# Batch 1's q and k loads, cut by runs into two or three transfers each

## The chip, the cores and the metric

The kernel runs on one core of one Trainium2 chip. The number that is compared is device time in microseconds for one execution; smaller is better. The core has a matrix engine (TensorE, PE in the profile; its weight loads are listed apart as PEld), a vector engine (VectorE, DVE), a scalar engine (ScalarE, ACT), GpSimd (POOL) and a sync engine (SyncE, SP). SP does no arithmetic here: it issues DMA transfers, one after the other, in the order of the program. Sixteen DMA engines move the data; every transfer in this trace reports its landing with sixteen signals on one semaphore, one from each DMA engine.

## What is computed

Inputs are q, k and v (8 batches, 8 heads, 576 positions, 64 wide, float32) and two weight matrices, `w_in` (512 x 2048) and `w_out` (2048 x 512).

```
scores = (q @ k.T) / 8 - slope[head] * |i - j|      for 0 <= i - j < 128, else masked
attn   = softmax(scores) @ v                         per batch and head
x      = attn, heads side by side                    4608 tokens x 512
h      = x @ w_in
out    = (h * clip(h + 3, 0, 6) / 6) @ w_out         4608 x 512, float32
```

## The kernel before

The heads of a batch are taken in pairs, so a batch has four groups g (batch 0 is g 0 to 3, batch 1 is g 4 to 7). For each group the kernel needs q and k transposed (64 x 576 per head) in bf16, computes scores for blocks of 128 by 128 on and beside the diagonal, exponentiates them on ACT, multiplies by v, normalises on DVE and transposes the result into `xT`. A block of 512 tokens of `xT` then goes through `moe_up` (640 matmuls in all at line 451, ACT at 470, DVE at 471) and `moe_down` (560 matmuls at line 501). The whole program is written out by hand: every engine's instructions stand in the order of the calls in `first_batch`, `second_batch` and `segment`, and pieces of the MoE work are put between the attention steps by `fill`.

The loads of q and k come in several forms. Batch 0 uses `load_run` (line 92): one transfer of 128 rows per group and tensor. Batches 1 and 2, and k of batch 3, use `load_double` (line 98). One call covers four heads of one tensor (half a batch, `dp` 0 or 1) with two transfers, e = 0 and e = 1. Each transfer has 64 runs of nine neighbouring positions for two heads; a run of one head is 9 x 64 float32 = 2304 bytes, contiguous in memory, and goes to one partition: partition 2a + i holds run a of the i-th of the two heads. So one transfer is 128 rows of 2304 bytes, 288 KB. Later batches and all of v use `load_tokens` (line 112), whose rows are 256 bytes.

What stands around batch 1's loads, all in `first_batch`:

- SP's queue is: q of batch 0 (k of batch 0 goes through ACT's queue), the five v transfers of batch 0, then batch 1's eight q and k transfers in the order k and q of dp 0, k and q of dp 1 (line 594), then the five v transfers of batch 1 (`load_tokens(1, "v")`), then batch 2's q and k (line 611).
- The transfers of SP and ACT share eight landing semaphores in rotation. In the trace a transfer that reuses a semaphore is issued only after the transfer that had it eight places earlier has landed: the first v transfer of batch 1 has the semaphore of the first k transfer, which landed at 18.76 us, and it is issued at 18.77 us; the second is issued at 21.27 us, after the landing of the second k transfer at 21.26 us.
- POOL casts batch 1's q and k to bf16 (`prepare_double`, line 227), eight casts in the order of the loads, each when its transfer has landed. Between the first and the second stands the load of the second quarter of `w_in` (`second_w_in`), which goes through POOL's own DMA queue. After the eighth cast POOL issues the third and fourth quarter (`load_w_in(2)`, `load_w_in(3)`).
- PE transposes the cast tiles in `wide_double` (line 254): q of dp 0 before the first full MoE block starts, k of dp 0 within it, k and q of dp 1 at the beginning of groups 4 and 5. The up projection of the first block (`fill`, line 451) goes through the quarters of `w_in` in order.
- Batch 1's v is cast on POOL by `cast_tokens(1, "v")` (lines 187 and 190) after group 5. Behind it on POOL stand the masks of groups 6 and 7 (line 354), the four loads of `w_out` (line 171) and batch 2's casts (`prepare_double(2, ...)`), whose first tiles PE transposes at line 242.

Of the kernel before, what the change touches and what calls it, by code (L numbers as in the profile page):

```python
# [18 lines left out]
def kernel(  # L19
# [10 lines left out]
    B, H, S, D = q.shape  # L30
# [10 lines left out]
    RP, RT = 64, 9  # L41
# [35 lines left out]
    ldbuf = [held.tile([128, NQ * H * D], FP32, name=f"ldbuf{i}") for i in range(4)]  # L77
# [7 lines left out]
    src_of = {"q": q, "k": k, "v": v}  # L85
# [4 lines left out]
    def load_run(g, nm, eng):  # L90
# [2 lines left out]
                      in_=src_of[nm][b, 2 * hp:2 * hp + 2, :, :].rearrange(  # L93
                          "e (p t) d -> (e p) (t d)", t=RT))

    def load_double(b, dp, nm, eng):
        for e in range(2):
            eng.dma_start(out=ldbuf["qk".index(nm)][:, ds((2 * dp + e) * RT * D, RT * D)],  # L98
                          in_=src_of[nm][b, ds(4 * dp, 4), :, :].rearrange(
                              "(i e) (a t) d -> e a i (t d)", e=2, t=RT)[e])  # L100
# [457 lines left out]
    def first_batch():  # L558
# [32 lines left out]
        for dp in range(2):  # L591
            for nm in "kq":
                load_double(1, dp, nm, nc.sync)
# [15 lines left out]
        for dp in range(2):  # L609
            for nm in "kq":  # L610
                load_double(2, dp, nm, nc.sync)
# [6 lines left out]
    def second_batch():  # L618
# [22 lines left out]
        for dp in range(2):  # L641
            load_double(3, dp, "k", nc.sync)
# [121 lines left out]
```

## Time and profile before

| | |
|---|---|
| device time, median of 2 runs | 325.73 us (325.59 to 325.86) |
| span of the profiled execution, first to last instruction | 325.3 us |
| TensorE clock granted | 1.000 |
| PE busy | 314.0 us (97%) |
| ACT / DVE / POOL busy | 198.4 / 173.7 / 141.4 us |
| batch 1's q and k: first issue, last landing | 12.52 us, 28.30 us |
| one such issue on SP: min / median | 0.54 / 0.6 us |

The runs are 0.3 to 0.6 us above the span: that is what lies around the first and the last instruction. Times within the kernel are counted from the start of the span. In lists of instructions an entry gives start and length, engine, line, operation and tiles; the bracket at the end is the time for which the engine stood idle before it and what ended that wait. In lists of waits the numbers are the total, how often, and the longest.

### The profile page before, as it was taken

How to read it: one execution, taken by the hardware profiler on the slowest of the kernel's cores; microseconds unless marked ns; L12 is line 12 of the kernel's file. 1: busy time of each engine (PE TensorE's matmuls, PEld its weight loads, DVE VectorE, ACT ScalarE, POOL GpSimd, SP SyncE). 2: the span in 40 equal slices, each digit the busy share in tenths (PEclk: the TensorE clock that was granted, in tenths of full speed). 3: DMA queues.
4: the chain of work that ended last, by engine and by line, in shares of the span. 5: the costliest groups of instructions: out<-in, count | busy, mean ns of one | idle time of the engine just before them, and what ended most of it. 6: DMA issues, size and time to landing. Idle time of an engine off the chain costs nothing.

```text
span 325.3 us, 7087 instructions
## 1 busy us (share of the span) xinstructions
PE 314.0 (97%) x2763; PEld 168.4 (52%) x2763; DVE 173.7 (53%) x338; ACT 198.4 (61%) x339; POOL 141.4 (43%) x249
## 2 busy tenths in 40 slices
PE   7869999999999999999999999999999999999996
PEld 6555465455555555555667655554554444444443
DVE  7657565554445655565555555554565544445510
ACT  4748877877766666666666666666666344244411
POOL 7446393495395566636663666462342000000000
PEclk9999999999999999999999999999999999999999
DMA  7999999799999999799989986931114100000112
GB/s 274 197 328 180 224 298 191 167 257 218 202 254 176 238 212 208 178 222 217 194 146 229 198 207 138 202 107 64 40 36 55 64 33 34 32 32 34 61 41 91
DMA packets 128065, 51.08 MB, mean 157 GB/s; under 512 B 115616, under 2 KB 119968, under 8 KB 128032
## 3 DMA queue, kind: packets, MB, share of 16 engines
q1 hardware_dynamic: 122800, 44.54, 63.4%
q0 software_dynamic: 4224, 4.19, 8.2%
q10 hardware_dynamic: 1008, 1.90, 1.6%
q8 instruction: 21, 0.34, 0.5%
q14 instruction: 12, 0.10, 0.1%
HBM read 36.70 MB, written 9.44 MB: 142 GB/s over the span
## 4 chain that ended last, share of the span: by engine, by line
PE 82%; DMA 7%; ACT 4%; SPq 3%; DVE 1%; issue 1%; POOL 0%; ACTq 0%
PE ops L501 37%; PE hps L451 34%; DMA ldbuf<-in_q_dram 3%; PE scd L296 2%; PE av L391 2%; DMA w_in_sb<-in_moe_w_in_dram 2%; SPq L112 2%; PE av L383 2%; DMA ldbuf<-in_k_dram 2%; ACT r L470 2%; SPq L98 1%; PE sco L328 1%; ACT xT L438 1%; PE ops L482 1%; PE tb L432 1%
## 5 line engine op out<-in xcount | busy, mean ns | idle before, releaser
L471 DVE SCALAR_TENSOR_TENSOR gbuf<-r,hps 128x512 bf16<-128x512 f32 x144 | 98.5, 686 | 104.8 <-ACT r L470 104.8
L470 ACT ACTIVATE r<-hps,bias 128x512 f32<-128x512 f32 x144 | 99.0, 689 | 82.1 <-PE hps L451 81.8
L451 PE MATMUL hps<-xT,w_in_sb 128*128 128x512 bf16 (+1 forms) x640 | 146.2, 358 | 2.7 <-DMA w_in_sb<-in_moe_w_in_dram 1.9
L501 PE MATMUL ops<-w_out_sb,gbuf 128*128 128x512 bf16 x560 | 138.6, 379 | 0.0
L451 PEld LDWEIGHTS <-w_in_sb 128*128 128x128 bf16 x640 | 58.8, 98 | 56.4 <-DMA w_in_sb<-in_moe_w_in_dram 3.0
L501 PEld LDWEIGHTS <-gbuf 128*128 128x128 bf16 x560 | 52.0, 98 | 56.0
L354 POOL TENSOR_SCALAR_AFFINE_SELECT pd<-pd 128x512 bf16<-128x512 bf16 x48 | 30.0, 633 | 58.4 <-ACT pd L351 58.4
L364 POOL TENSOR_SCALAR_AFFINE_SELECT po<-po 128x512 bf16<-128x512 bf16 x48 | 30.3, 634 | 25.5 <-ACT po L361 24.7
L351 ACT ACTIVATE pd<-scd,bias_d 128x512 bf16<-128x512 f32 x48 | 32.1, 685 | 2.6 <-POOL vbuf L187 2.6
L361 ACT ACTIVATE po<-sco,bias_o 128x512 bf16<-128x512 f32 x48 | 33.2, 692 | 0.0
L510 DVE COPY osb<-ops 128x512 f32<-128x512 f32 x33 | 22.7, 688 | 18.7 <-PE ops L501 18.1
L194 POOL CAST tbuf<-ldbuf 128x512 bf16<-128x512 f32 (+1 forms) x45 | 25.6, 611 | 3.9 <-DMA qTb<-tbuf 3.1
L402 DVE TENSOR_TENSOR avs<-av,rc 128x384 bf16<-128x384 f32 (+1 forms) x48 | 23.6, 491 | 1.6
L391 PEld LDWEIGHTS <-pd 128*128 128x128 bf16 x192 | 14.3, 97 | 8.2 <-issue 0.9
L438 ACT COPY xT<-tb 128x576 bf16<-128x576 bf16 x13 | 8.3, 638 | 16.7 <-PE tb L432 16.7
L383 PE MATMUL av<-vbuf,po 128*128 128x65 bf16 x192 | 18.0, 193 | 0.0
L391 PE MATMUL av<-vbuf,pd 128*128 128x65 bf16 x192 | 17.3, 194 | 0.3 <-ACT kTb L244 0.3
L187 POOL CAST vbuf<-ldbuf 128x1024 bf16<-128x1024 f32 x14 | 14.3, 1040 | 5.2 <-DMA ldbuf<-in_v_dram 5.2
L383 PEld LDWEIGHTS <-po 128*128 128x128 bf16 x192 | 14.3, 98 | 3.0 <-DVE avs L402 0.5
L227 POOL CAST pr<-ldbuf 128x576 bf16<-128x576 f32 x20 | 12.8, 668 | 6.6 <-PE tb L432 2.5
L367 ACT ACTIVATE p4buf<-sco,bias_d 128x64 bf16<-128x64 f32 x48 | 15.7, 327 | 0.0
L296 PEld LDWEIGHTS <-kTb 64*128 64x128 bf16 x256 | 7.2, 94 | 14.1 <-issue 10.6
(96 smaller groups left out, 227.3 us busy)
## 6 DMA issues: line engine op xcount, KB each, us to landing
out_dram<-osb SPq DMA_DIRECT2D x33, 256.0 KB, 2.4
ldbuf<-in_v_dram SPq DMA_DIRECT2D x32, 256.0 KB, 5.6
ldbuf<-in_q_dram SPq DMA_DIRECT2D x20, 256.0 KB, 4.7
ldbuf<-in_k_dram SPq DMA_DIRECT2D x16, 256.0 KB, 4.8
ldbuf<-in_q_dram SPq DMA_DIRECT2D x12, 288.0 KB, 7.8
ldbuf<-in_k_dram SPq DMA_DIRECT2D x12, 288.0 KB, 8.1
w_in_sb<-in_moe_w_in_dram POOLq DMA_DIRECT2D x4, 512.0 KB, 9.8
w_out_sb<-in_moe_w_out_dram POOLq DMA_DIRECT2D x4, 512.0 KB, 11.3
```

The lines of the kernel that those rows point to most:

```text
L194: nc.gpsimd.tensor_copy(out=tbuf[:m, :, j, :], in_=s[:m, j, :, :].rearrange("p (i e) d -> p i (e d)", e=2))
L351: nc.scalar.activation(out=pd[:, e, :, :].rearrange("p j c -> p (j c)"), in_=sc[:, e, :], func=ACT.Exp, bias=bias_d[:, h:h + 1], scale=scale)
L354: nc.gpsimd.affine_select(out=pd[:, e, :, :], in_=pd[:, e, :, :], pattern=[[0, 4], [1, 128]], channel_multiplier=-1, base=0, compare_op=AL ...
L361: nc.scalar.activation(out=po[:, e, :, :].rearrange("p j c -> p (j c)"), in_=sc[:, e, :], func=ACT.Exp, bias=bias_o[:, h:h + 1], scale=scale)
L364: nc.gpsimd.affine_select(out=po[:, e, :, :], in_=po[:, e, :, :], pattern=[[0, 4], [-1, 128]], channel_multiplier=1, base=-1, compare_op=A ...
L383: nc.tensor.matmul(out_av, lhsT=po[:, e, qt % 4, :], rhs=vb[:, qt - 1, h, :], start=True, stop=False)
L391: nc.tensor.matmul(out_av, lhsT=d, rhs=vb[:, qt, h, :], start=(qt == 0), stop=True)
L402: nc.vector.tensor_tensor(out=st[g, "avs"][:, qts[0]:qts[0] + nq, :, :], in0=av[:, 0:nq, :, 0:D], in1=rc[:, 0:nq, :, :].to_broadcast([128, ...
L451: nc.tensor.matmul(hps[:, lo:hi], lhsT=w_in_sb[:, ks, ts(ms, 128)], rhs=xT[:, ks, ds(src, hi - lo)], start=(ks == 0), stop=(ks == n_ks - 1))
L470: nc.scalar.activation(out=r6, in_=hps, func=ACT.Relu, bias=bias3[:, 0:1], scale=1.0 / 6.0)
L471: nc.vector.scalar_tensor_tensor(out=gts[nt][:, ms, :], in0=r6, scalar=1.0, in1=hps, op0=ALU.min, op1=ALU.mult)
L501: nc.tensor.matmul(ops[nt, sub], lhsT=gts[nt][:, ms, ts(sub, 128)], rhs=w_out_sb[:, ms, :], start=(ms == 0), stop=(ms == n_ms - 1))
```

## The change

`load_double` gets a table for batch 1. For each of the eight transfers it gives two or three numbers that add up to 64, and the transfer is replaced by that many, each for so many consecutive runs (and twice as many partitions). The rows, their 2304 bytes, their places in memory and in `ldbuf`, and the total are as before. Eight transfers become nineteen. Batches 2 and 3 keep the old form, and no other line differs.

```
+    PARTS = {(0, "k", 0): (60, 4), (0, "k", 1): (52, 12), (0, "q", 0): (44, 20),
+             (0, "q", 1): (56, 8), (1, "k", 0): (55, 9), (1, "k", 1): (50, 9, 5),
+             (1, "q", 0): (48, 13, 3), (1, "q", 1): (48, 10, 6)}
+
     def load_double(b, dp, nm, eng):
+        if b == 1:
+            for e in range(2):
+                lo = 0
+                for n in PARTS[dp, nm, e]:
+                    eng.dma_start(
+                        out=ldbuf["qk".index(nm)][ds(2 * lo, 2 * n),
+                                                  ds((2 * dp + e) * RT * D, RT * D)],
+                        in_=src_of[nm][b, ds(4 * dp, 4), :, :].rearrange(
+                            "(i e) (a t) d -> e a i (t d)", e=2, t=RT)[e, lo:lo + n])
+                    lo += n
+            return
         for e in range(2):
             eng.dma_start(out=ldbuf["qk".index(nm)][:, ds((2 * dp + e) * RT * D, RT * D)],
```

## The prediction, made before the changed kernel was run

> **What bounds the kernel now.** I read the page's slices first, then the chain that ended last, then the waits and the order of instructions around the changed loads.
>
> ```profile
> PE   7869999999999999999999999999999999999996
> DMA  7999999799999999799989986931114100000112
> ```
>
> Each digit is a fortieth of the span, 8.1 us. PE is full from the fifth slice on, so a microsecond can only be gained or lost in about the first 50 us, and what is lost there moves the rest. The same is said in numbers by the busy times per stretch:
>
> ```profile
> 18.10:28.30 10.20, 7.85 (x105) 5.58 (x106) 5.89 (x11) 4.90 (x8) 5.38 (x9) 1.00 1.12 305
> 28.30:36.30 8.00, 6.94 (x66) 3.45 (x64) 6.79 (x9) 7.59 (x12) 5.53 (x8) 1.00 0.98 165
> 60.00:325.30 265.30, 261.58 (x2044) 136.01 (x2041) 136.08 (x255) 156.47 (x280) 107.14 (x186) 1.00 0.66 138
> ```
>
> The first number behind the stretch is its length, the second PE's busy time. From 18.1 to 36.3 us PE idles 3.4 us; in the 265 us after 60 it idles 3.7. In the early stretch the DMA engines are full (shares 1.12 and 0.98). The chain there, with start and length:
>
> ```profile
> 17.55 10.75 DMA ldbuf<-in_q_dram
> 28.30 0.05 issue
> 28.36 0.61 POOL pr L227
> 28.97 7.28 DMA w_in_sb<-in_moe_w_in_dram
> 36.25 0.05 issue
> 36.30 1.05 PE hps L451 x4
> ```
>
> The eighth transfer of the changed group lands at 28.30, POOL casts it, issues the third quarter of `w_in`, and PE waits for that until 36.30. This is the first gate. Its waits:
>
> ```profile
> PE hps L451 <- DMA w_in_sb<-in_moe_w_in_dram: 1.9, 2, 1.1
> PE tp L254 <- POOL pr L227: 0.8, 1, 0.8
> ```
>
> The 1.9 are 1.1 at 22.2 (first quarter) and 0.8 at 36.3 (third); the 0.8 of L254 is the cast of dp 0's q. So at most 1.9 + 0.8 = 2.7 us of PE idling hang on these transfers. A second gate is on POOL:
>
> ```profile
> 40.08 1.04 POOL L187 CAST vbuf<-ldbuf 128x1024 bf16<-128x1024 f32 x1 [4.17 <-DMA ldbuf<-in_v_dram]
> ...
> 46.94 2.50 POOL L227 CAST pr<-ldbuf 128x576 bf16<-128x576 f32 x4
> ```
>
> POOL waits 4.17 us for batch 1's fourth v transfer and then has no gap until 51.9. The second of those four casts ends at about 48.2, and PE transposes its tile at 48.35. A later v moves that too.
>
> **What holds the last q back.** The trace has sixteen landing signals for each transfer. Those of the eighth are at 23.98 to 24.93 for thirteen engines and at 26.55, 27.17 and 28.30 for three. So the chain waits for three late engines, 1.6 to 4.3 us behind the first. Single 16384-byte packets of an instruction queue, at 10.65, 18.08 and 24.19 us, take 0.93 to 1.31 us each on some engine; v of batch 0 already lands with one straggler (14.09 against 12.81 us). I take these packets for part of the cause. Which engines are late the trace doesn't say.
>
> **Rows per engine.** Before: 1024 rows, 64 on each engine. For the parts I assume that a transfer runs in equal shares on the largest number of engines up to 16 that divides its runs, and always from the same end. Then 60 runs go to 15 engines with 8 rows each, 4 to 4 with 2, and so on: 52/12 to 13 and 12 engines, 44/20 to 11 and 10, 56/8 to 14 and 8, 55/9 to 11 and 9, 50/9/5 to 10, 9 and 5, 48/13/3 to 16, 13 and 3, 48/10/6 to 16, 10 and 6. The fullest engine gets 10 + 10 + 12 + 10 + 12 + 14 + 10 + 10 = 88 rows; ten of the engines get 74 to 88; the thin end gets 58, 40, 38, 28, 20 and 12. No transfer of the trace shows fewer than 16 engines, so this is a choice; the other ends are 64 everywhere (shares rotate) and 88 with the late engines among the full ones. The Trainium skill, DMA: Bandwidth & Descriptors, "Why a DMA increments its semaphore by 16 and not by 1", gives this division and the lowest-numbered engines; no run so far shows it. Its "Rules for kernel authors" advises one 128-partition transfer over a split one and all 16 engines; by that rule alone the sum would be a loss, like mine.
>
> **The last landing, by rows.** A 2304-byte row takes 93 ns (median) when rows have the engine alone. From 23.57 us the second quarter of `w_in` comes in, and on the engine that is late between 20.3 and 21.7 us a 1024-byte packet (96 to 98 ns) starts every 0.18 us: the two queues alternate. A prompt engine that ended at 23.98 has 24 rows more: 24 x 0.093 = 2.2 us without alternation, 24 x (0.093 + 0.096) = 4.5 with it. It ends between 26.2 and 28.5. I take 28.5, as the alternation is seen. If the late engines are the thin ones they have 36 to 52 rows less, 3.3 to 4.8 us, and are no longer last.
>
> **The last landing, by issues.**
>
> ```profile
> 12.52 1.42 SPq L98 DMA_DIRECT2D ldbuf<-in_k_dram  x2
> ...
> 18.77 11.95 SPq L112 DMA_DIRECT2D ldbuf<-in_v_dram  x5
> SPq L112 <- DMA ldbuf<-in_k_dram: 4.9, 4, 2.1
> ```
>
> Eight issues take 12.52 to 18.1: one each 0.72 us. Nineteen put the last at 12.52 + 18 x 0.72 = 25.5. An issue of a few rows isn't in the trace: the cheapest of any DMA takes 0.33 us (output stores), with 0.1 between it gives 20.3, but then the rotation of eight semaphores (the 4.9 us above) holds: the ninth waits for the first (18.3), the seventeenth for the ninth (23 to 24). So the last goes out between 24.2 and 26; a transfer with the engines to itself lands 2.6 us behind the end of its issue (issued 63.34 to 63.95, landed 66.61), 0.75 of it for 8 rows. That gives 26.8 to 29.2, about 28.6 with 0.72. Both ways agree on 28.5 to 28.6: **0.3 us later than 28.30**.
>
> **What follows from it.** Gate one: the third quarter of `w_in` is issued 0.3 later and lands at 36.55, +0.3. What comes earlier in the first half is covered: with prompt engines alone, the first quarter of `w_in` (fifteen engines by 20.71, the last at 22.17) and dp 0's q (42 rows instead of 32 on the full engines, 21.8 + 0.9 = 22.7 against 23.33) come 0.6 to 1.4 us earlier, but PE then stands longer before the later quarters. Gate two: batch 1's v is issued behind the nineteen, from about 26.2 instead of 18.77. The DMA engines do the same work until 40.6, but the full ones 2.2 us more of it: the prompt engines that gave the last v signals at 38.76 give them at about 41.0 against 40.59 from the late ones, and some idling in the thin end's favour isn't made up; I put the fourth v at 41.0 instead of 40.02, +1.0. With no gap on POOL behind it the cast of batch 2's k comes 1.0 later, 0.15 of which PE has spare: +0.9 at 48.3. This holds the 0.3 of gate one, it isn't added. Extra waits of a POOL cast for two or three transfers are 17 ns each and nothing. The loads of batch 2 slip too; they landed by 46.76, its first four by 43.46, with casts from 46.94, so 2 us of slip is hidden. `w_out` is needed from 53.6 and 64.2 us, landed by 49.33 and 60.04: 4 us to spare.
>
> Sum: span 325.3 + 0.9 = 326.2; the runs lie about 0.4 above the span (325.73), so **326.6 us**.
>
> **Rivals.**
>
> *The late engines stand at the full end.* For it: nothing ties the three to either end. The latest then has 24 rows more; some 7 of them still alternate with `w_in` and 17 don't: 7 x 0.19 + 17 x 0.093 = 2.9, and up to 0.4 by a further instruction packet, so the last q lands at about 31.6, the third quarter at 39.5: +3.3, 329.0. It decides as soon as a late engine has more than 64 rows. The Trainium skill, DMA: Bandwidth & Descriptors, "Latency and other measured facts", calls engines 7 and 15 usually slower; by it 15 would gain and 7 (80 rows) lose, which lies between this and my forecast.
>
> *The balance works.* Short transfers are issued quickly and `w_in` doesn't hold the rows: last landing 26.2, third quarter at 34.2, and PE, ready at 35.5 and some 0.9 earlier by the earlier first quarter and q, saves 0.8 + 0.9 = 1.7 if v isn't later: 324.0. Against it: alternation and gate two.
>
> *The parts don't change the shares* (they rotate, or all use sixteen). Then the three late engines stay late, the bytes per engine too, and only the issues count: +0 at gate one, +0.5 at gate two: 326.2.
>
> **How the numbers follow.** Forecast 0.45, late engines at the full end 0.2, balance 0.25, shares unchanged 0.1. The forecast's own bounds (26.8 to 29.2 for the last q, v on time or 2 us late) give 325.2 to 327.8. The range goes from most of the balance case to just past the rival at 329.0: 324.2 to 329.4. Two per cent, about what a measurement of this kernel can tell from no change, are 6.5 us: no gain comes near it with 2.7 us of idling to win; a loss would need the late engines full and v and `w_in` late together. Faster 0.01, same 0.94, slower 0.05.
>
> **What would show it.** Right: nineteen issues from 12.5 to about 25.5; PE's first wait for `w_in` gone from 22.2; eighth cast near 28.6; PE's wait at 36.3 to 36.8; the cast of v at about 41. Wrong: the last cast near 26 and no wait at 36 (balance), or near 31 (wrong end); short issues well under 0.5 us; or a v that lands by 40, so that gate two is nothing.

## The result, and the profile after

The changed kernel takes **330.42 us** (two runs, 330.09 and 330.75) against 325.73: ratio 1.0145, 95% interval 1.0121 to 1.0169. It is slower by 4.7 us; that is within 2%, but outside the predicted range of 324.2 to 329.4. One execution of e3 below (332.22 us), more than 1.5% above the quickest of that kernel, is left out of its ratio.

The slices of the page after, PE, PE's granted clock and the DMA engines:

```profile
PE   7869899999999999999999999999999999999996
PEclk9997999999999999999999999999999999999999
DMA  7997999999989999699989996941013100000112
```

In PE only the fifth slice differs from before (8 instead of 9), and the clock, 9 throughout before, has a 7 in the fourth. From the first down-projection matmul (line 501 before, 516 after) to the end both traces take the same time: 271.6 us before, 271.9 after. That first matmul stands at 53.64 before and at 56.49 after, so all of the traces' difference (spans 325.3 and 328.4) arises ahead of it.

SP's order of issues after, with start, length and count:

```profile
12.24 3.58 SPq L105 DMA_DIRECT2D ldbuf<-in_k_dram  x4
15.86 3.49 SPq L105 DMA_DIRECT2D ldbuf<-in_q_dram  x4
19.45 4.20 SPq L105 DMA_DIRECT2D ldbuf<-in_k_dram  x5
23.70 5.74 SPq L105 DMA_DIRECT2D ldbuf<-in_q_dram  x6
29.48 4.10 SPq L127 DMA_DIRECT2D ldbuf<-in_v_dram  x5
```

The nineteen issues fill 12.24 to 29.44; the last goes out at 28.69. The last six take 5.74 us, 1.1 of it a wait for the landing of the eleventh transfer (28.67). v is issued from 29.48 instead of 18.77.

The chain after, at the first gate (pieces with start and length):

```profile
21.24 7.44 DMA ldbuf<-in_k_dram
28.69 2.24 DMA ldbuf<-in_q_dram
...
31.08 0.61 POOL pr L242
31.69 7.41 DMA w_in_sb<-in_moe_w_in_dram
...
39.15 1.05 PE hps L466 x4
```

It is the chain of before with one link ahead of it: transfer 11, issued at 21.24, lands at 28.67 and lets the nineteenth go out; that lands at 30.93, POOL casts it, issues the third quarter of `w_in`, and PE waits until 39.15 instead of 36.30. From there to the first down-projection matmul it is 17.34 us in both traces (36.30 to 53.64, 39.15 to 56.49), so the 2.85 us of the first gate are all by which that matmul is later.

PE's busy time per stretch (length, then PE's busy time; the last three numbers are clock, DMA share, GB/s):

```profile
18.10:28.30 10.20, 7.38 (x90) 5.13 (x86) 5.63 (x10) 3.25 (x6) 4.05 (x7) 0.84 0.97 242
28.30:36.30 8.00, 7.40 (x70) 3.90 (x69) 5.05 (x8) 7.02 (x11) 4.75 (x8) 0.98 0.91 175
36.30:44.00 7.70, 6.57 (x57) 2.96 (x55) 3.73 (x5) 6.47 (x10) 4.14 (x6) 1.00 1.17 262
```

In the first stretch the core moves 242 GB/s instead of 305: before, all eight transfers are issued by 18.1 us, after only seven of nineteen have begun to be. POOL's order shows the casts and the second gate:

```profile
26.28 0.67 POOL L242 CAST pr<-ldbuf 128x576 bf16<-128x576 f32 x1 [1.72 <-DMA ldbuf<-in_k_dram]
29.28 1.37 POOL L242 CAST pr<-ldbuf 128x576 bf16<-128x576 f32 x2 [2.34 <-DMA ldbuf<-in_k_dram]
31.08 0.67 POOL L242 CAST pr<-ldbuf 128x576 bf16<-128x576 f32 x1 [0.43 <-DMA ldbuf<-in_q_dram]
...
40.31 1.04 POOL L202 CAST vbuf<-ldbuf 128x1024 bf16<-128x1024 f32 x1 [1.89 <-DMA ldbuf<-in_v_dram]
43.02 0.61 POOL L205 CAST vbuf<-ldbuf 64x512 bf16<-64x512 f32 x1 [1.67 <-DMA ldbuf<-in_v_dram]
```

The fourth v transfer is late by 0.2 us only (40.31 against 40.08), the fifth by 2 (43.02 against 41.06), which is less than the 2.85 that PE has already lost: the second gate no longer binds.

Of the 4.7 us between the medians the two traces show 3.1. The trace of before has a span of 325.3; all later runs lie 1.7 us above their spans, and the kernel before varied from 325.0 to 327.8 in them, with spans from 323.3 to 326.0. If that holds for the trace of before too, it belongs to an execution of about 327.0, later than its median. I have no trace of it at 325.6, and where it is 1.3 us quicker there stays open.

### The profile page after: what moved, and what is told of

Its sections match the earlier page's. It is cut to its first block, busy times and chain, and to the rows that moved or that the text cites. A ratio compares the mean times of both kernels' runs of the same rounds, so it can differ in the third digit from the quotient of the medians.

```text
span 328.4 us, 7105 instructions
## 1 busy us (share of the span) xinstructions
PE 315.5 (96%) x2763; PEld 169.1 (51%) x2763; DVE 173.5 (53%) x338; ACT 198.6 (60%) x339; POOL 141.3 (43%) x249
## 4 chain that ended last, share of the span: by engine, by line
PE 84%; DMA 5%; ACT 5%; DVE 3%; issue 1%; POOL 0%; POOLq 0%
PE ops L516 37%; PE hps L466 34%; PE scd L311 3%; PE av L406 2%; DMA ldbuf<-in_k_dram 2%; DMA w_in_sb<-in_moe_w_in_dram 2%; PE av L398 2%; ACT r L485 1%; PE sco L343 1%; ACT xT L453 1%; PE tb L447 1%; PE ops L497 1%; PE w L168 1%; DMA ldbuf<-in_q_dram 1%; ACT kTb L259 1%
## 5 line engine op out<-in xcount | busy, mean ns | idle before, releaser
L379 POOL TENSOR_SCALAR_AFFINE_SELECT po<-po 128x512 bf16<-128x512 bf16 x48 | 30.4, 634 | 27.4 <-ACT po L376 26.5
L209 POOL CAST tbuf<-ldbuf 128x512 bf16<-128x512 f32 (+1 forms) x45 | 25.5, 611 | 1.4 <-issue 1.4
```

What stands on the lines that cost most here:

```text
L209: nc.gpsimd.tensor_copy(out=tbuf[:m, :, j, :], in_=s[:m, j, :, :].rearrange("p (i e) d -> p i (e d)", e=2))
L379: nc.gpsimd.affine_select(out=po[:, e, :, :], in_=po[:, e, :, :], pattern=[[0, 4], [-1, 128]], channel_multiplier=1, base=-1, compare_op=A ...
```

## The experiments

Two theories stood first. **SHARES**: the loss comes from the uneven shares, some DMA engines with 88 rows. **COUNT**: it comes from the number of transfers, by the issue queue and the rotation of eight semaphores (an entry waits for the landing of the one eight places ahead), whatever their shares. Two more are about what COUNT acts through: **PACE**, the queue issues its last transfer too late, and **HOLD**, the second quarter of `w_in` runs ahead of the rows that are still to come. **HIDDEN** says that the half-rate stretch of PE's clock at 25.1 us costs nothing.

| kernel | transfers | last issue | last q landed | third quarter landed | first down-projection | us | ratio (95%) |
|---|---|---|---|---|---|---|---|
| before, its trace | 8 | 17.6 | 28.30 | 36.25 | 53.64 | 325.73 | |
| after | 19 | 28.69 | 30.93 | 39.10 | 56.49 | 330.42 | 1.0145 (1.0121–1.0169) |
| e0 before again | 8 | 17.5 | 28.04 | 36.65 | 54.04 | 326.13 | 1.0008 (0.9987–1.0029) |
| e1 equal shares | 19 | 27.74 | 29.99 | 39.13 | 56.52 | 329.90 | 1.0148 (1.0066–1.0231) |
| e6 equal shares | 16 | 25.36 | 31.21 | 39.48 | 58.33 | 328.84 | 1.0106 (1.0053–1.0159) |
| e7 one engine spared | 16 | 26.79 | 31.63 | 40.73 | 59.65 | 332.96 | 1.0220 (1.0178–1.0261) |
| e2 only dp 0 cut | 12 | 23.00 | 31.19 | 38.43 | 55.82 | 329.36 | 1.0095 (1.0065–1.0125) |
| e3 only dp 1 cut | 15 | 25.58 | 29.64 | 36.50 | 53.90 | 331.41 | 1.0119 (1.0044–1.0195) |
| e4 quarter later | 19 | 28.18 | 32.59 | 41.40 | 61.29 | 332.32 | 1.0200 (1.0126–1.0273) |
| e9 before + 11 small | 8 (+11) | – | 26.48 | 32.90 | 55.81 | 329.53 | 1.0111 (1.0072–1.0151) |
| e10 quarter last | 19 | 28.78 | 31.11 | 42.81 | 65.8 | 339.4 | one run |
| e11 e1, quarter last | 19 | 27.39 | 29.80 | 42.45 | 64.38 | 338.06 | one run |
| e12 PE filled | 19 | 28.89 | 31.24 | 40.20 | 59.17 | 331.58 | 1.0176 (1.0139–1.0213) |
| e13 before, quarter early | 8 | 17.5 | 27.12 | 32.13 | 51.67 | 326.00 | 0.9987 (0.9965–1.0008) |

Columns three to six are of one trace each, the time is the median of all runs of that kernel. The ratio on record compares with runs of the kernel before that were measured alongside; it isn't the quotient of two medians of the table. A trace need not be of a median execution: those of e4, e6 and e12 are of the slowest (334.90, 331.67 and 332.78 us), those of e3 and e13 of the quickest (327.29 and 325.02).

**e0: the kernel before again.** No edit; which part of its late last q is the kernel's own?

> The kernel before itself, for a trace from the same kind of run as the others. Time 325.1 to 327.4, no difference. If the stragglers belong to the kernel, the eighth q lands again 3 to 4 us behind the prompt engines, at 27 to 28.5; if they belong to one execution, it lands within 2 us of them.

The last q landed at 28.04 with one engine 2.2 us behind the next (25.87); in the trace of before three were late (28.30). Late engines belong to this kernel's early stretch; which they are, these two traces don't say.

**e1: nineteen transfers in equal shares.** The lengths are multiples of 16, so all run on sixteen engines and each engine keeps 64 rows:

```
+    PARTS = {... five of the eight: (48, 16); the other three: (32, 16, 16)}
```

> Nineteen transfers in the same places, but in parts of 48 and 16 or of 32, 16 and 16 runs, so that all run on sixteen engines with 64 rows on each. Theory COUNT (nineteen issues at 0.8 us each and the rotation of eight landing semaphores make the last q late): as the changed kernel, 329.5 to 331 us, last q landed at 29.5 to 31. Theory SHARES (88 rows on the full engines make it late): within 1 us of the kernel before, 325.5 to 327, last q near 28.5.

The loss is the same, 1.0148, without uneven shares: COUNT, not SHARES. It isn't the clock's either: at a granted clock of 0.999 and 1.000 two of e1's executions took 330.21 and 328.94. SP's order:

```profile
12.00 2.84 SPq L103 DMA_DIRECT2D ldbuf<-in_k_dram  x4
14.89 2.54 SPq L103 DMA_DIRECT2D ldbuf<-in_q_dram  x4
17.53 5.21 SPq L103 DMA_DIRECT2D ldbuf<-in_k_dram  x5
22.79 5.52 SPq L103 DMA_DIRECT2D ldbuf<-in_q_dram  x6
```

The first eight issues take 5.4 us, 0.67 each with their gaps, close to before; in the next eleven there are waits, 2.9 us in three: the tenth goes out at 19.34, right behind the second's landing at 19.32, the eleventh at 20.91 behind 20.85, the nineteenth at 27.74 behind 27.73. That is the rotation of eight semaphores. Its last issue is only 1 us ahead of after's, which has dearer issues and one such wait of that size.

**e6 and e7: sixteen transfers.** e6 cuts each of the eight into (32, 32), on sixteen engines; e7 into (60, 4), on fifteen and four.

> All eight transfers in two parts of 32 runs: sixteen transfers, 64 rows on each engine. COUNT: sixteen issues at 0.8 us end at 25, last q near 28.5 to 29.5, 1.5 to 3.5 us over the kernel before (327.2 to 329.2). SHARES: as the kernel before, 325.5 to 326.5.

> All eight transfers in parts of 60 and 4 runs: sixteen transfers, nothing on the last engine, 64 rows on eleven and 80 on four. COUNT: as the run with two parts of 32, within 0.7 us. SHARES: 0.5 to 1.5 us slower than that run, by 16 rows of 0.093. If one late engine is the last one and nothing else counts: faster than the kernel before by 0.5 to 1.5 us.

e6's time fell where COUNT put it, 1.1% instead of 1.5, but its last q, at 31.21, is later than the 28.5 to 29.5 expected. e7 has e6's count and is 4 us slower, which neither expectation had. Three things differ in the traces. Its issues take 0.87 and 0.67 us instead of 0.6, so that its last one goes out at 26.79 instead of 25.36. One late engine brings the third quarter to 40.73, where the other fifteen have signalled by 38.35; in e6 the last is 0.28 behind the next. And its clock has two stretches at half rate (24.9 and 41.96) against one (39.31); but an e7 execution at 0.994, which is one such stretch, still took 332.19. How the 4 us divide is open, and so is what the uneven shares of e7 have to do with it; to spare an engine is not free even at an equal count.

**e2 and e3: one half of the change.** The table for dp 0 alone (twelve transfers) and for dp 1 alone (fifteen), (64,) for the rest.

> The table for dp 0 alone, dp 1 in four whole transfers: twelve. Theory COUNT by the eight landing semaphores: the twelfth waits for the fourth, which lands at 21.4, so it goes out near 21.5 and nothing runs dry; last q at 27 to 29, 326 to 327.5 us. Theory that the split of dp 0 itself costs (late first casts): half of the loss, 327.5 to 329.

> The table for dp 1 alone, dp 0 in four whole transfers: fifteen. COUNT: the fifteenth waits for the seventh, issued with the others behind whole transfers; last q at 28.5 to 30, 327 to 329.5 us, more than with dp 0 split. Per transfer it would be 7 of 11 added ones, some 3 us: 328.5.

e2 missed what the rotation alone would give. Its last issue is at 23.00, and yet its last q lands at 31.19: the four transfers of dp 1, issued from 20.42, meet the second quarter of `w_in`, which is in service from 23.1, and land at 24.33, 27.81, 30.38 and 31.19. Here HOLD sets the end, not PACE, and three late engines add the last 1.6 us: thirteen have signalled the last q by 29.59. e3 is slower than the 327 to 329.5 expected. Its four runs are in two groups: 327.29 with the clock at 1.000, and 331.2 to 332.2 with 0.990 to 0.995; its trace is of the first. That one execution lies between the kernel before's median and its latest (326.13 and 327.54 in e0), so a cost of dp 1's parts at full clock isn't shown; the 1.2% comes with a clock that falls, and where it falls in those executions, no trace says. The trace has one more lesson. Its last q lands 1.3 us later than in the trace of before, and its third quarter only 0.25 later, because that took 6.10 us from issue to landing. In the other traces (but for e10 and e11, where the second quarter goes right ahead of it) it took 5.76 (e9) to 8.38 us (e1), 7.28 before and 7.41 in after. So a late q isn't passed on to PE microsecond by microsecond.

**e4: the second quarter of `w_in` after dp 0's four casts**, instead of after the first.

```
-        prepare_double(1, 0, (P, P), early=second_w_in)
+        prepare_double(1, 0, (P, P))
+        second_w_in()
```

> The changed kernel with the second quarter of w_in issued after the four casts of dp 0 instead of after the first. Theory HOLD (the second quarter, from 21.9 us on, holds the later transfers back): the transfers of dp 1 land 1 to 2 us earlier, the last q at 29 to 29.5, 1 to 2 us faster than the changed kernel, 328.4 to 329.4. COUNT without HOLD: the last q stays at 30.9; time as the changed kernel or up to 1.5 us slower by the later quarter, 330 to 332.

This missed: 332.32, not a gain. The four runs are in two groups, 330.37 and 330.54 (after: 330.42) at a clock of 0.999, and 334.11 and 334.90 at 0.990; the trace is of the last. In it dp 1's k is all there at 26.2 instead of 29.17, so the quarter had held it. But the quarter now runs from 26.5 to 29.5 and holds five of the six q transfers instead (landed 30.64 to 32.59). Counted in half microseconds, it starts 92, 98, 102 and 101 of its 1024-byte packets from 27.0 to 29.0, and the rows 2, 0, 0 and 0.

**e10 and e11: the second quarter after all eight casts**, in after and in e1. PE has to wait for it (8.2 us in e10, 9.8 in e11), so the time says nothing; the landing of the last q does.

```
         prepare_double(1, 1, (P, P))
+        second_w_in()
         load_w_in(2)
```

> The changed kernel with the second quarter of w_in issued only after all eight casts, so that nothing of w_in is in the way of the q and k rows after the first quarter. Read is the landing of the last q, not the time, which is worse because PE then waits for that quarter (333 to 337 us). Theory PACE (nineteen issues at 0.8 to 0.87 us each bound it): last issue at 27.5 to 28.3, last q at 29.5 to 30.3 against 30.9. Theory HOLD (the second quarter holds the rows): last q at 28.5 or before.

> The same move of the second quarter in the kernel with nineteen transfers of 16 or more runs, whose issues take 0.64 each. PACE: 12.0 + 18 x 0.64 = 23.5 for the last issue, and with it the last q at 26 to 26.5. ROTATION (each waits for the one eight before): some waits of 1 us, last issue at 25 to 26.5, last q at 27 to 28.5. In both cases clearly before the 30.0 with the quarter in the way, if HOLD is right; 29.5 or later if it isn't.

With no quarter in the way the last q landed at 31.11 (after: 30.93) and at 29.80 (e1: 29.99), both on PACE's side of the expectations (e10 later than its 29.5 to 30.3). So nineteen transfers are late without the quarter too: in e10 the DMA engines' busy share from 22 to 30 us is 0.53, against 1.02 in the trace of before, which means that they wait for the queue. But the two traces don't show that the quarter has no part in it. e10's order is that of after, with 0.84 us per transfer, and it has a wait of 1.25 us that after doesn't have, of the ninth (20.70) for the landing of the first (20.64, one engine 1.7 us behind the next):

```profile
12.44 3.59 SPq L105 DMA_DIRECT2D ldbuf<-in_k_dram  x4
16.07 3.32 SPq L105 DMA_DIRECT2D ldbuf<-in_q_dram  x4
20.70 4.14 SPq L105 DMA_DIRECT2D ldbuf<-in_k_dram  x5
24.89 4.64 SPq L105 DMA_DIRECT2D ldbuf<-in_q_dram  x6
```

Without that wait its last issue would go out at about 27.5, and its last q would land 2.3 us later, at about 29.9; that is my estimate from these numbers. It is 1.6 us behind the 28.30 of before. The other 1.0 us in after comes with its wait for the eleventh transfer, which was 7.4 us under way with the second quarter beside it, and 4.07 us in e10. So PACE carries about 1.6 of the 2.6 us, and HOLD reaches the last issue through the rotation. In e1 the last issue waits for the eleventh too (6.8 us under way, 3.2 in e11); how e1's loss divides stays open, because e11 was held up otherwise.

It was held up by two single issues of 1.45 and 1.53 us that end with no landing; there is one of 1.62 in e1, of 1.71 in e6 and of 1.30 in e12. Each of these overlaps a 16384-byte packet of an instruction queue (from 18.28 and 22.04 in e11, 25.37 in e1, 22.24 in e6, 24.60 in e12). That SP then waits for its own instructions is a guess: other issues overlap such a packet and aren't longer.

From the last issue to the last landing it is 2.2 to 2.4 us in after, e1, e10, e11 and e12 (nineteen), and 4 to 8 us in e2, e3, e6 and e7, whose queues end earlier and whose rows then wait.

**e9: the kernel before with eleven small transfers** (16 rows of 128 bytes each, into a tile that nothing reads) between the q and k and v: SP's queue gets nineteen, the rows stay as before.

```
+        for i in range(11):
+            nc.sync.dma_start(out=spare[0:16, ts(i, D // 2)], in_=moe_w_in[0:16, ts(i, D // 2)])
         load_tokens(1, "v")
```

> The kernel before with eleven tiny transfers (16 rows of 128 bytes each into an unused buffer) issued between batch 1's eight whole q and k transfers and its v. The last q stays where it is in the kernel before. COUNT acts on v alone here: v goes out at 25 to 28 instead of 18.8. If the loss of the change comes from the late q (gate one): 325.5 to 326.7. If it comes from the late v (gate two): 328 to 330.

Here gate one is early (last q 26.48, third quarter 32.90) and the kernel still loses 1.1%; what its trace shows of it is at gate two:

```profile
18.09 10.11 SPq L596 DMA_DIRECT2D spare<-in_moe_w_in_dram  x11
28.24 10.54 SPq L113 DMA_DIRECT2D ldbuf<-in_v_dram  x5
```

```profile
PE tp L243 <- POOL pr L228: 2.1, 1, 2.1
```

v is issued from 28.24, its fourth transfer is cast at 41.40, and PE waits 2.1 us for batch 2's cast behind it (the second fence is of e9's list of waits). So the two gates stand close behind one another: eleven more entries in this queue cost time at the first in after and e1, and at the second here.

**e12: after, with PE kept busy at 23.4** by thirty further warm-up matmuls, so that its clock stays up.

```
         back(3)
+        warm_up(30)
         wide_double(1, 0, "q", V)
```

> The changed kernel with thirty 128-column matmuls on PE where it waits 1.9 us for dp 0's q. Theory CLOCK (the half-rate stretch from 25.1 to 28.5 is on the path): mean clock 1.000 and 1 to 1.7 us less than the changed kernel, 328.7 to 329.4. Theory HIDDEN (PE waits for the cast of dp 1's k and for the third quarter behind it anyway): clock 1.000 and 329.8 to 330.8.

PE's order in after, and then in e12:

```profile
24.61 0.71 PE L269 MATMUL tp<-ident,pr 128*128 128x128 bf16 x9 [1.90 <-POOL pr L242]
25.13 1.90 PE L466 MATMUL hps<-xT,w_in_sb 128*128 128x512 bf16 x4
...
30.01 0.68 PE L269 MATMUL tp<-ident,pr 128*128 128x128 bf16 x9 [0.60 <-POOL pr L242]
```

```profile
23.44 1.84 PE L168 MATMUL w<-ident 128*128 128x128 bf16 x30
25.12 0.67 PE L269 MATMUL tp<-ident,pr 128*128 128x128 bf16 x9
25.62 1.03 PE L466 MATMUL hps<-xT,w_in_sb 128*128 128x512 bf16 x4
...
30.14 0.68 PE L269 MATMUL tp<-ident,pr 128*128 128x128 bf16 x9 [1.92 <-POOL pr L242]
```

The four matmuls take 1.03 us instead of 1.90, the stretch at half rate is gone from there, and PE then waits 1.92 us for dp 1's k instead of 0.60. The time isn't better: 331.58, some 1 us above what HIDDEN expected, with another stretch at half rate at 40.75 in the trace; its ratio's interval overlaps that of after, and its quickest execution, 331.25, is still above the 328.7 to 329.4 of CLOCK. HIDDEN was right in its point: what the slow clock at 25 us costs is covered by the late k.

**e13: before, with the third quarter issued behind dp 1's first cast** instead of its last, the one edit that attacks the first gate without more transfers.

```
-        prepare_double(1, 1, (P, P))
-        load_w_in(2)
+        prepare_double(1, 1, (P, P), early=lambda: load_w_in(2))
```

> The kernel before with the third quarter of w_in issued after the first cast of dp 1 instead of after the fourth (3.5 us earlier); q and k loads whole as in the kernel before. If the third quarter alone gates: 0.8 to 1.5 us faster than the kernel before, 324.2 to 325. If v (second gate) is as late or later by it: no change or up to 1.5 us slower.

The quarter lands at 32.13 instead of 36.25 and PE's wait for it is gone, yet the time is the same (0.9987, 0.9965 to 1.0008), not the 0.8 to 1.5 us less that were expected of this gate alone. The chain there goes through the quarter before it and then through ACT:

```profile
18.62 9.52 DMA w_in_sb<-in_moe_w_in_dram
28.14 0.05 issue
28.19 1.04 PE hps L451 x4
...
38.60 1.39 ACT r L470 x2
```

PE goes on with the second quarter's landing (28.14), and from 35.4 the chain is mostly ACT's. So the 0.8 us of the first gate before the change could not have been won by this gate alone, and no version tried here is measurably quicker than the kernel before.

## Why the prediction was wrong, by its steps

**The last landing, by issues: this is the step that failed.** It priced an issue at 0.72 us, left the waits of the rotation out of its sum, and put the last issue at 25.5; it went out at 28.69. Two terms were wrong:

- *The price.* 0.72 was the mean of issues on sixteen engines with the gaps between them. In after, an issue on sixteen engines takes 0.61 to 0.63 us, on three to eight 0.70 to 0.75, on nine to thirteen 0.78 to 0.86, and the first one, on fifteen, 1.02 (the later ones on fifteen take 0.87 to 0.89 in e7). With gaps and without waits that is 0.85 per transfer: 12.24 + 18 x 0.85 = 27.5. I took "the cheapest of any DMA", 0.33, as the lower bound for a transfer of a few rows; the step asked how many rows a transfer has, where the price went by the number of engines that it runs on: lowest on sixteen, dearer on every other number that ran. (e9's eleven entries, 16 rows of 128 bytes on sixteen engines, do take 0.31 to 0.42 apart from the first; what makes those cheap no run separates.)
- *The rotation.* I counted it as a bound for cheap issues and left it out of the sum. In after it costs another 1.1 us: the nineteenth waits for the landing of the eleventh, 27.5 + 1.1 = 28.6, measured 28.69. In e1, with cheap issues, it is the larger part (2.9 us of waits, where 12.0 + 18 x 0.64 would be 23.5 and the last goes out at 27.74).

The tail behind the end of the last issue, 2.6 us in the step, took 1.5 (29.44 to 30.93), which made up for part of it. So 25.5 + 3.1 = 28.6 became 28.69 + 2.24 = 30.93. The upper end that I gave this step, 29.2, was too low by 1.7 for the same two reasons.

**The last landing, by rows** agreed with that, and by accident: it had neither the price of an issue nor the rotation. Its alternation of one packet of `w_in` with one row doesn't hold for the second quarter in after and e4: while that is in service the rows nearly stop. In after it starts 78, 80, 95 and 76 packets per half microsecond from 23.0 to 25.0, the rows 9, 11, 1 and 14; in e4, above, it is plainer still. The Trainium skill, DMA: Bandwidth & Descriptors, "Queues, rings and completion order", says that a DMA engine goes round the queues and takes from each, in turn, a packet of typically 9 to 17 descriptors and at most 64. By my estimate from that figure a quarter, with 512 pieces of 1024 bytes and so 32 on each engine, could pass as one block only near the upper limit, and e4's counts look like such a block. What the quarter held back reached the last issue through the eleventh transfer, by about 1 us, which this way of counting didn't have. Two ways to one number are no check when both miss the queue.

**Rows per engine** held as to the number of engines. In after a transfer of few engines shows one signal 1.1 to 1.4 us after its issue begins and then as many as the division gives engines (15 for 60 runs, 4 for 4, down to 3), and the sum over each semaphore comes out exactly. The Trainium skill, DMA: Bandwidth & Descriptors, "Why a DMA increments its semaphore by 16 and not by 1", gives that division, and the early signal for the engines that aren't used; the traces agree. That it is always the same end that goes without, no trace shows. The first quarter of `w_in` landed at 20.19 instead of 22.17, and PE's first matmul on it went from 22.21 to 21.17. That looks like the thin end at work, but with equal shares it landed at 20.25 (e1) and 20.15 (e6), so the shares aren't its cause. It bought nothing: dp 0's last q cast ends at 24.56 instead of 24.05, dp 1's first at 26.95 instead of 24.89.

**What holds the last q back** was right for the kernel before (e0 has a late engine too). In after the nineteenth transfer has all its signals 2.24 us after its issue; late engines act one link earlier, on the eleventh: eight of its ten have signalled by 27.58, the last two come at 28.11 and 28.67, and the nineteenth waits for that.

**Gate one** was the right gate with the right chain behind it (cast 0.6, load 7.4), but +2.85 instead of +0.3. That the load took 7.4 us in after and 7.3 before is in part luck: over the traces it varied by 2.6 us (see e3). **Gate two**, which carried the forecast with +0.9, did not bind in after: the fourth v was 0.2 late, not 1.0. e9 shows that the mechanism is real, at 2.1 us, once gate one is out of the way. **Extra waits**, the order on SP and the loads of batch 2 and `w_out` cost nothing, as said.

**The sum** put 0.4 us around the span; it is 1.7 in every later run, and the trace of before, if the same holds for it, was of a late execution. With 1.7 the sum would have been 327.9, from a trace that is itself 1.3 us above the median.

**The rivals.** "The late engines at the full end" gave 329.0 with a last q at 31.6, near the measured 30.93, by a mechanism that the loss doesn't need: in e1, with equal shares, it is the same. "The balance works" needed short issues, and they are long. "The parts don't change the shares" put the issues alone at +0.5 us; e1, which is that case, lost 1.5%. No rival was the one that happened: SP's queue itself as the bound of the last landing, with a price above 0.72 and a wait for a transfer still under way.

## What to carry to other kernels

A load that is cut into parts is paid for at the queue that issues it: count the issues up to the one that the chain waits for, take the price from a transfer on as many engines as the part will use (here 0.6 us on sixteen and 0.67 to 0.89 on fewer), and add a wait for every entry whose semaphore is still in flight eight places earlier. If the queue's end plus one transfer (here 2.2 us from the last issue) lies behind the landing of before, no balance of bytes can bring that landing forward. And follow the queue on to what is issued behind it: here v, which cost PE a wait of 2.1 us in e9.

## What the runs showed of the hardware that was not expected

- **An issue on fewer engines than sixteen is dearer.** But it isn't dearer the fewer they are: 0.53 to 0.70 us on sixteen engines (e1, e6, before), 0.67 to 0.72 on four and eight, 0.74 to 0.76 on three, five and six, 0.77 to 0.86 on nine to thirteen (once 0.98, on eleven in e3), 0.82 on fourteen, 0.87 to 0.89 on fifteen. Left out are the long issues named under e11, the seventh of after (0.99), which overlaps such a packet too, and the first of each batch, which is dearer: 0.76 to 0.80 on sixteen, 1.01 to 1.02 on fifteen.
- **A loaded quarter can pass as a block.** In e4, from 27.0 to 29.0, 2 rows of another queue start beside 393 packets of the quarter; whoever issues such a load decides which rows wait. It isn't so everywhere: in e2, from 24.0 to 25.0, 79 packets of the quarter and 62 rows start.
- **PE's clock falls for 3.41 us at a time.** The records of after have half rate from 25.13 to 28.55, following a stretch in which PE had waited 1.90 us for a cast; such stretches are 3.41 us long, or 6.83 in e4 and 10.24 in e10 and e11, where PE stood still for longer. The Trainium skill, TensorE: Matmul & The Clock Gate, Part 1, gives a window of 3413 ns and half rate for an idle one; the length agrees. In after the 3.41 us ahead of 25.13 had work in them on both sides of the wait, so here a window that was idle in part was enough. Where such a stretch comes late (from 39.31, 41.96 and 40.75 in e6, e7 and e12), the first down-projection matmul stands 18.8 to 18.9 us behind the point at which PE goes on with the third quarter: about 1.5 us more than the 17.34 of before and e1, which have none there. Where it comes at 25 us that distance is 17.34 (after) and 17.12 (e2).
